# Three DMA queues instead of two for the backward part of a cached-attention decode kernel

## The chip, the cores and the metric

The kernel runs on one core of one Trainium2 chip. The time is device microseconds for one launch, and the number compared is the median of several executions. One further execution was recorded by the hardware profiler; all rows of a profile shown below come from such a recording. Engines are named as the profile names them: PE does matrix products (PEld loads their weights), DVE the element-wise work, ACT copies and activations, POOL (GpSimd) some small copies and some DMA issues, SP (SyncE) DMA issues only. Sixteen DMA engines move all data between device memory and the on-chip buffer.

## The reference

The forward pass is one decode step of a transformer block: layer norm, attention of one query per batch row and head against a cache of 4096 keys and values, then a gated feed-forward part. The kernel must give the output and, for a given gradient of the output, the gradients of eight inputs. Cut to what matters here:

```python
B, Sq, D = 4, 1, 512;  H, Sk, Dh = 32, 4096, 128          # bfloat16 throughout
q      = (layernorm(x) @ wq).reshape(B, Sq, H, Dh).transpose(0, 2, 1, 3)
scores = einsum("bhqd,bhkd->bhqk", q, k_cache) * Dh ** -0.5
p      = softmax(scores)
o      = einsum("bhqk,bhkd->bhqd", p, v_cache)
h      = x + o.transpose(0, 2, 1, 3).reshape(B, Sq, H * Dh) @ wo
out    = h + swiglu(layernorm(h), w1, w3, w2)
# returned: out and the vjp of out for x, k_cache, v_cache, wq, wo, w1, w3, w2
```

For each of the B x H = 128 heads, the gradient of the values is the outer product of p (4096 long) and the gradient dO of that head's output (128 long). The gradient of the keys is the outer product of dS and q, where dS = p * (V dO - c) * scale, with one number c per head. K, V, dK and dV are each 128 heads of 4096 x 128 numbers, 1 MB per head, so reading K once and V twice and writing dK and dV once is nearly all of the 708 MB that the kernel moves.

## The kernel before

The kernel has a forward part (up to about 690 us), a short middle part (the feed-forward part and its gradient), and a backward part that runs over the 128 heads, s = 0 to 127. The order of instructions on every engine is the order of the program text; each engine works through its own queue in that order and stops at an instruction whose wait isn't met.

On-chip memory is cut into 23 slots of 1 MB (lines 103 to 120). `Slot(...)` takes the oldest free slot from a list, and `give()` puts it back at the end. A slot that is taken again is written only when its last use has ended; for a slot that was stored, this means that the store has landed.

One head in the backward part goes as follows.

- `load_V2` (line 789) issues the load of a head's V (line 793) from SP. In the backward part the slots of V form a ring of seven (`NV2`, `vring`): `front` gives a slot back to the ring when the products that read it have been issued, and `prefetch` (line 1168), at the start of each step of the loop, loads the next head into it. Nine heads are loaded ahead before the loop starts (lines 801 and 873).
- `front(s)` (line 1140) transposes V of head s on PE in four groups of eight blocks (`V_T`, line 760), ACT copies each group back into the same slot (line 761), and PE multiplies it with dO in 32 small products (line 1148, tile `dP_ps`). `front` also asks POOL for `P_pairs` (line 1138), a copy of p in the form that DVE reads.
- `grad_V(s)` (line 773) lets DVE form the outer product p x dO in a slot `gv` (line 766) and stores it to `out_3`, the gradient of V, from POOL (line 777).
- `grad_K(s)` (line 1154) lets DVE form dS (lines 1158 and 1161) and the outer product dS x q in a slot `gk` (line 766) and stores it to `out_2`, the gradient of K, from POOL (line 1165).

In the loop (line 1175) the order is: prefetch, `front(s + 1)`, `grad_V(s + 1)`, `grad_K(s)`, and from step 2 on a piece of side work (`step`): first the rest of dO (lines 1103 to 1116), from step 21 on `side_work` (lines 947 to 1098), which makes the gradients of x and the five weight matrices. The side work issues some transfers of its own: loads of wq (line 977) and w2 (line 499) from SP, rearrangements of a few rows (lines 969, 1032 and 1072) from ACT, and the stores of the weight gradients from POOL.

Each transfer signals its end on one of sixteen semaphores that the compiler deals out in turn: eight for transfers issued from POOL, and eight shared by those issued from SP and ACT. A transfer that is dealt a semaphore waits, on the engine that issues it, until the transfer that had this semaphore before has landed. So at most eight transfers of each kind are under way at a time.

Of the kernel before, what the change touches and what calls it, by code (L numbers as in the profile page):

```python
# [24 lines left out]
def kernel(  # L25
# [22 lines left out]
    nc = tc.nc  # L48
# [35 lines left out]
    def bh_of(s):  # L84
        return s % B, s // B

    def rows_of(ap):
        return ap.rearrange("(p j) d -> p j d", p=P)

    def cache_head(ap, s):  # L90
        b, h = bh_of(s)
        return rows_of(ap[b, h])
# [82 lines left out]
    def ones_window(col):  # L175
# [11 lines left out]
                          in_=rowg[:, None, :, None].to_broadcast([P, 4, 8, 4]))  # L187
# [409 lines left out]
    def step(k, n=1):  # L597
        for _ in range(n):
            next(units[k], None)
# [150 lines left out]
    V2s, VTs = {}, {}  # L750
# [14 lines left out]
    def outer(dst, col2, row):  # L765
        nc.vector.tensor_tensor(  # L766
            out=dst.rearrange("p j (r t) -> p j r t", t=2),
            in0=col2[:, :, None, :].to_broadcast([P, SJ, Dh // 2, 2]),
            in1=row.rearrange("p (r t) -> p r t", t=2)[:, None, :, :].to_broadcast([P, SJ, Dh // 2, 2]),
            op=ALU.mult,  # L770
        )

    def grad_V(s):
        b, h = bh_of(s)
        gv = Slot("gv")
        outer(gv.heads(), P2s.pop(s), reps["rdo", s // REP][:, s % REP, :])
        nc.gpsimd.dma_start(out=rows_of(out_3[b, h]), in_=gv.heads())  # L777
        if s > 1:
            gv.give()
        else:  # L780
            first_gv.append(gv)
# [4 lines left out]
    vring = deque()  # L786
    nv = {"next": 0}

    def load_V2():
        s = nv["next"]  # L790
        if s < NH:
            V2s[s] = Slot("V2", vring if vring else free)
            nc.sync.dma_start(out=V2s[s].heads(), in_=cache_head(A_v_cache, s))
            nv["next"] += 1

    with ExitStack() as cm:
# [4 lines left out]
        while free:  # L801
            load_V2()
# [70 lines left out]
        while len(free) > 1:  # L873
            load_V2()
# [48 lines left out]
    with ExitStack() as c2:  # L923
# [216 lines left out]
        def front(s):  # L1140
            if s % REP == 0:
                replicate(s)
            if s not in VTs:
                V_T(s, psT)
            VT = VTs[s].heads()
            dP_ps = psD.tile([P, SJ], FP32, name="dP_ps", tag="dP")
            for j in range(SJ):
                nc.tensor.matmul(dP_ps[:, j:j + 1], lhsT=VT[:, j, :], rhs=dOT_bf[:, s:s + 1], start=True, stop=True)  # L1148
            sl = VTs.pop(s)
            (vring if len(V2s) + len(VTs) + len(vring) < NV2 else free).append(sl.i)  # L1150
            P_pairs(s + 2)
            bwd[s] = dP_ps

        def grad_K(s):
            b, h = bh_of(s)
            dP_ps = bwd.pop(s)
            t = bw3.tile([P, SJ], FP32, tag="dSt", name="dSt")
            nc.vector.tensor_scalar(out=t[:], in0=dP_ps[:], scalar1=c_rep[:, s:s + 1], scalar2=scale,  # L1158
                                    op0=ALU.subtract, op1=ALU.mult)
            dS2 = bw3.tile([P, SJ, 2], BF16, tag="dS2", name="dS2")  # L1160
            nc.vector.tensor_tensor(out=dS2[:], in0=t[:, :, None].to_broadcast([P, SJ, 2]),
                                    in1=P_all[:, s, :, None].to_broadcast([P, SJ, 2]), op=ALU.mult)
            gk = Slot("gk")
            outer(gk.heads(), dS2, reps["rq", s // REP][:, s % REP, :])
            nc.gpsimd.dma_start(out=rows_of(out_2[b, h]), in_=gk.heads())  # L1165
            gk.give()

        def prefetch():
            while nv["next"] < NH and vring:
                load_V2()  # L1170


        O0, S0 = 2, 21
# [1 line left out]
        for s in range(NH):  # L1175
            prefetch()
            if s + 1 < NH:
                if s + 1 not in V2s and s + 1 not in VTs:
                    load_V2()
                if s == 0:  # L1180

                    first_gv[0].give()
                front(s + 1)
                if s > 0:
                    grad_V(s + 1)
            grad_K(s)
            if s == 0:
                first_gv[1].give()
            if s >= S0:
                step("s", 1 if s < S0 + 38 else 3)  # L1190
            elif s >= O0:
                step("o")
# [31 lines left out]
```

## Time and profile before

| | |
|---|---|
| median of 4 executions | 1724.37 us (1723.57 to 1726.14) |
| the profiled execution's own time | 1724.0 us |
| its span, first to last instruction | 1721.7 us |
| moved | 707.87 MB, mean 411 GB/s over the span |
| of that, written | 282.34 MB |
| busy: PE, DVE, ACT, POOL | 77%, 73%, 56%, 26% of the span |
| copies of transposed V on ACT, line 761 | 512 of 1016 ns |
| outer products on DVE, line 766 | 125 + 128 of 2293 ns |
| issue of a dK or dV store on POOL | 256 of 533 ns |

The profile's rows of DMA queues name them by what issues them: `hardware_dynamic` q1 holds what SP issues, q10 what ACT issues, `software_dynamic` q0 what POOL issues. The DMA row in the list of 40 slices (43 us each) is the mean busy share of the sixteen DMA engines, in tenths. The span and the execution's own time differ by 2.3 us of start and end outside the instructions.

### The profile page before, as it was taken

To read this page: it belongs to the slowest core of one execution; us is meant where nothing else is said; L and a number is where in the kernel's file an instruction comes from. 1 tells how busy PE (TensorE), PEld (TensorE's weight loads), DVE (VectorE), ACT (ScalarE), POOL (GpSimd) and SP (SyncE) were. 2 spreads that over 40 slices of the span, in tenths; PEclk is the share of its full clock that TensorE was granted. 3 is DMA by queue.
4 is the path that set the end of the run, shared out by engine and by line. 5 is a ranking of instruction groups with operands and counts; after the bars stand their busy time and mean duration, and the time that the engine had idled before them with its cause. 6 is when DMAs were issued, how large, how long until landed. Compare 5 with 4: busy or idle time off the path is not lost.

```text
span 1721.7 us, 44279 instructions
## 1 busy us (share of the span) xinstructions
PE 1320.2 (77%) x19124; PEld 1117.2 (65%) x19124; DVE 1255.7 (73%) x1389; ACT 960.1 (56%) x1470; POOL 440.6 (26%) x808
## 2 busy tenths in 40 slices
PE   5888888888888888887687788767638777887760
PEld 4777776666667666876677777767636555665660
DVE  5899899899998997676766676665566456655582
ACT  3455444444454444677555555547637657777660
POOL 1221222222222231221122333322233232222221
PEclk8999999999999999666756655656866565555665
DMA  9999999999999999999999999999999999999996
GB/s 397 419 418 419 419 419 419 418 419 418 411 418 406 418 403 395 377 424 418 414 418 415 417 413 415 416 419 416 422 423 410 421 411 415 416 416 415 415 419 286
DMA packets 101867, 707.87 MB, mean 411 GB/s; under 512 B 11284, under 2 KB 15392, under 8 KB 17704
## 3 DMA queue, kind: packets, MB, share of 16 engines
q1 hardware_dynamic: 62272, 422.60, 59.5%
q0 software_dynamic: 39008, 282.37, 40.0%
q8 instruction: 150, 2.46, 0.5%
q14 instruction: 45, 0.37, 0.1%
q10 hardware_dynamic: 392, 0.07, 0.0%
HBM read 422.59 MB, written 282.34 MB: 409 GB/s over the span
## 4 chain that ended last, share of the span: by engine, by line
DMA 50%; PE 4%; DVE 4%; issue 2%; ACT 2%; POOL 0%; ACTq 0%; POOLq 0%; DVEq 0%
DMA out_dram<-gv 28%; DMA out_dram<-gk 22%; DVE gv L766 1%; DVE gk L766 1%; ACT V L761 1%; PE pt_tps L760 1%; PE M_ps L433 1%; DVE PK L418 1%; PE pt_w L562 0%; ACT Pn L397 0%; ACTq L1072 0%; PE kP_ps L443 0%; PE gps L942 0%; PE gu_ps L833 0%; PE pt_wo L571 0%
## 5 line engine op out<-in xcount | busy, mean ns | idle before, releaser
L761 ACT COPY V<-pt_tps 128x1024 bf16<-128x1024 bf16 x512 | 492.4, 1016 | 186.4 <-PE pt_tps L760 127.6
L760 PE MATMUL pt_tps<-ident_b,V 128*128 128x128 bf16 x4096 | 445.2, 289 | 60.4 <-ACT V L761 55.0
L760 PEld LDWEIGHTS <-V 128*128 128x128 bf16 x4096 | 393.8, 136 | 124.1 <-issue 116.5
L766 DVE TENSOR_TENSOR gv<-P,reps 128x4096 bf16<-128x4096 bf16 x125 | 286.7, 2293 | 207.2 <-DMA out_dram<-gv 74.4
L766 DVE TENSOR_TENSOR gk<-dS,reps 128x4096 bf16<-128x4096 bf16 x128 | 293.4, 2292 | 104.6 <-DMA out_dram<-gk 47.8
L433 PE MATMUL M_ps<-PK,Vn 128*128 128x130 bf16 x4096 | 287.7, 223 | 43.4 <-DMA Vn<-in_A_v_cache_dram 43.0
L418 DVE TENSOR_TENSOR PK<-Kn,PK 128x4096 bf16<-128x4096 bf16 x128 | 292.4, 2284 | 32.8 <-POOL PK L414 32.5
L433 PEld LDWEIGHTS <-Vn 128*128 128x128 bf16 x4096 | 254.6, 100 | 64.0 <-DMA Vn<-in_A_v_cache_dram 55.9
L325 DVE STREAM_TRANSPOSE KT<-Kn 128x512 f32<-128x512 f32 (+1 forms) x321 | 250.7, 797 | 0.3 <-issue 0.2
L320 ACT COPY KT<-pt_tps 128x1024 bf16<-128x1024 bf16 x128 | 129.5, 1012 | 189.1 <-PE pt_tps L319 153.1
L1148 PE MATMUL dP_ps<-dOT_bf,V 128*128 128x1 bf16 x4096 | 145.4, 165 | 108.3 <-DVE dSt L1158 58.6
L1148 PEld LDWEIGHTS <-V 128*128 128x128 bf16 x4096 | 137.5, 102 | 124.2 <-issue 64.4
L1165 POOL DMA_DIRECT2D out_dram<-gk x128 | 68.2, 533 | 392.9 <-DMA out_dram<-gk 144.5
L331 POOL TENSOR_TENSOR W<-qrep,wmask 128x128 bf16<-128x128 bf16 x128 | 123.2, 963 | 82.4 <-PE S_ps L351 67.8
L777 POOL DMA_DIRECT2D out_dram<-gv x128 | 68.4, 534 | 285.3 <-DVE dSt L1158 98.6
L414 POOL COPY PK<-P_all 128x64 bf16<-128x64 bf16 x128 | 32.6, 254 | 422.1 <-ACT P_all L408 419.1
L1138 POOL COPY P<-P_all 128x64 bf16<-128x64 bf16 x125 | 118.9, 951 | 0.0
L408 ACT COPY P_all<-pt_P 32x64 bf16<-32x64 bf16 x256 | 52.1, 203 | 60.0 <-PE pt_P L404 57.7
L319 PE MATMUL pt_tps<-ident_b,Kn 128*128 128x128 bf16 x1024 | 80.0, 222 | 0.0
L443 PE MATMUL kP_ps<-PK,onesw 128*32 128x512 bf16 x1024 | 79.5, 387 | 0.0
L319 PEld LDWEIGHTS <-Kn 128*128 128x128 bf16 x1024 | 61.6, 99 | 25.7 <-issue 25.6
L1129 ACT CAST reps<-rep_ps 128x512 bf16<-128x512 f32 x62 | 36.4, 587 | 72.7 <-PE rep_ps L1126 70.3
(237 smaller groups left out, 1349.6 us busy)
## 6 DMA issues: line engine op xcount, KB each, us to landing
Kn<-in_A_k_cache_dram SPq DMA_DIRECT2D x128, 1024.0 KB, 15.7
Vn<-in_A_v_cache_dram SPq DMA_DIRECT2D x128, 1024.0 KB, 16.0
V<-in_A_v_cache_dram SPq DMA_DIRECT2D x128, 1024.0 KB, 10.9
out_dram<-gv POOLq DMA_DIRECT2D x128, 1024.0 KB, 27.3
out_dram<-gk POOLq DMA_DIRECT2D x128, 1024.0 KB, 27.4
wq<-in_A_wq_dram SPq DMA_DIRECT2D x8, 1024.0 KB, 10.9
out_dram<-gw POOLq DMA_DIRECT2D x6, 896.0 KB, 27.9
wo<-in_A_wo_dram SPq DMA_DIRECT2D x4, 1024.0 KB, 12.4
```

Source lines behind the costliest of these rows:

```text
L319: nc.tensor.transpose(pt[:, i, :], Kn[:, c * GW + i, :], ident_b[:])
L320: nc.scalar.copy(out=KT[:, c * GW:(c + 1) * GW, :], in_=pt[:])
L325: nc.vector.transpose(out=KT[:, c * w_:(c + n) * w_], in_=Kn[:, c * w_:(c + n) * w_])
L331: nc.gpsimd.tensor_tensor(out=W[:, hl], in0=qrep[:, :, s:s + 1].to_broadcast([P, 4, 32]), in1=wmask[:, hl, None, :].to_broadcast([P, 4, 32 ...
L418: nc.vector.tensor_tensor(out=PK[:, :, 0:Dh].rearrange("p j (r t) -> p j r t", t=2), in0=Ks[s].heads().rearrange("p j (r t) -> p j r t", t=2),
L433: nc.tensor.matmul(hold["M"][:], lhsT=Vn[:, j, :], rhs=PK[:, j, :], start=(j == 0), stop=(j == SJ - 1))
L443: nc.tensor.matmul(hold["kP"][32 * q:32 * (q + 1), :, :], lhsT=ones_window(w), rhs=PK[:, j0:j0 + 4, 0:Dh], start=(w == 0 and c == 0), stop ...
L760: nc.tensor.transpose(pt[:, i, :], v[:, g * GW + i, :], ident_b[:])
L761: nc.scalar.copy(out=v[:, g * GW:(g + 1) * GW, :], in_=pt[:])
L766: nc.vector.tensor_tensor(out=dst.rearrange("p j (r t) -> p j r t", t=2), in0=col2[:, :, None, :].to_broadcast([P, SJ, Dh // 2, 2]), in1=r ...
L1138: nc.gpsimd.tensor_copy(out=P2s[s][:], in_=P_all[:, s, :, None].to_broadcast([P, SJ, 2]))
L1148: nc.tensor.matmul(dP_ps[:, j:j + 1], lhsT=VT[:, j, :], rhs=dOT_bf[:, s:s + 1], start=True, stop=True)
```

## The change

In the backward part three engines issue the large transfers, one kind each: the V loads that the loop asks for go from SP to ACT, the dK stores go from POOL to SP, and the dV stores stay on POOL. The nine V loads ahead of the loop stay on SP, since `load_V2` keeps SP as its default.

```diff
-    def load_V2():
+    def load_V2(eng=nc.sync):
         s = nv["next"]
         if s < NH:
             V2s[s] = Slot("V2", vring if vring else free)
-            nc.sync.dma_start(out=V2s[s].heads(), in_=cache_head(A_v_cache, s))
+            eng.dma_start(out=V2s[s].heads(), in_=cache_head(A_v_cache, s))
             nv["next"] += 1
...
             gk = Slot("gk")
             outer(gk.heads(), dS2, reps["rq", s // REP][:, s % REP, :])
-            nc.gpsimd.dma_start(out=rows_of(out_2[b, h]), in_=gk.heads())
+            nc.sync.dma_start(out=rows_of(out_2[b, h]), in_=gk.heads())
             gk.give()
 
         def prefetch():
             while nv["next"] < NH and vring:
-                load_V2()
+                load_V2(nc.scalar)
...
                 if s + 1 not in V2s and s + 1 not in VTs:
-                    load_V2()
+                    load_V2(nc.scalar)
```

PE and DVE keep their instructions and order. ACT gains 119 load issues, POOL loses 128 store issues, and SP loses the 119 loads and gains the 128 stores.

## The prediction

> **What bounds the kernel now.** I read the page's slices first, then its queues and its chain, then stretches of the span, then the waits of the queues that the change touches.
>
> ```profile
> span 1721.7 us, 44279 instructions
> ...
> DMA  9999999999999999999999999999999999999996
> GB/s 397 419 418 419 419 419 419 418 419 418 411 418 406 418 403 395 377 424 418 414 418 415 417 413 415 416 419 416 422 423 410 421 411 415 416 416 415 415 419 286
> ...
> q1 hardware_dynamic: 62272, 422.60, 59.5%
> q0 software_dynamic: 39008, 282.37, 40.0%
> ...
> DMA 50%; PE 4%; DVE 4%; issue 2%; ACT 2%; POOL 0%; ACTq 0%; POOLq 0%; DVEq 0%
> ```
>
> The DMA row is 9 until the last slice, and the two queues together fill 99.5% of sixteen engines' span. The chain that ended last is half DMA: stores of gv and gk, each holding a slot that DVE needs next. No compute engine is above 77%. So the time is bytes divided by the rate of the DMA engines, plus a start and an end. No byte changes, so the change can only act on the rate, on the end, or by letting the DMA engines run dry. The stretches, from the table of windows (busy times of PE, PEld, DVE, ACT and POOL, then clock, DMA share, GB/s):
>
> ```profile
> 86.00:430.00 344.00, 295.00 (x4904) 241.29 (x4901) 315.38 (x417) 175.24 (x385) 84.98 (x204) 0.99 1.01 419
> 731.00:1634.00 903.00, 677.16 (x8548) 584.49 (x8546) 576.04 (x485) 567.97 (x672) 247.62 (x358) 0.62 1.01 417
> 1290.00:1634.00 344.00, 266.19 (x3028) 207.80 (x3027) 206.19 (x167) 239.61 (x311) 94.59 (x136) 0.58 1.01 415
> 1640.00:1700.00 60.00, 29.82 (x456) 26.67 (x454) 43.94 (x36) 27.86 (x30) 13.89 (x31) 0.64 1.01 418
> 1700.00:1704.00 4.00, 0.00 (x0) 0.00 (x0) 0.00 (x0) 0.00 (x0) 0.06 (x1) 0.50 1.02 420
> 1704.00:1708.00 4.00, 0.00 (x0) 0.00 (x0) 0.00 (x0) 0.00 (x0) 0.00 (x0) 0.50 0.63 266
> 1708.00:1718.50 10.50, 0.00 (x0) 0.00 (x0) 0.00 (x0) 0.00 (x0) 0.00 (x0) 0.50 0.17 71
> ```
>
> Two losses are to be seen. Forward, with SP's loads alone, the rate is 419 GB/s; backward, with SP's loads and POOL's stores, 417 (415 in its second half) at the same full share. And the engines don't finish together: at 1704 the share falls from 1.02 to 0.63, then to 0.17, until about 1718. Some DMA engines end 14 us after the first ones, all of them working on POOL's stores, since the last V load is issued at 1640. The waits, and the issue times (minimum, median, maximum in ns):
>
> ```profile
> SPq L793 <- PE dP_ps L1148: 815.0, 112, 23.5
> SPq L977 <- DMA out_dram<-gk: 47.2, 3, 20.1
> SPq L977 <- DMA out_dram<-gv: 15.4, 1, 15.4
> POOL out_dram L1165 <- DMA out_dram<-gk: 144.5, 45, 4.7
> POOL out_dram L777 <- DMA out_dram<-gv: 98.1, 44, 4.1
> L793 SPq DMA_DIRECT2D V<-in_A_v_cache_dram x128: 327/328/1868, 676.4 to 1640.0; - x128
> V<-in_A_v_cache_dram SPq DMA_DIRECT2D x128, 1024.0 KB, 10.9
> out_dram<-gv POOLq DMA_DIRECT2D x128, 1024.0 KB, 27.3
> out_dram<-gk POOLq DMA_DIRECT2D x128, 1024.0 KB, 27.4
> ```
>
> SP is idle at the dP products: V loads run as far ahead as their ring allows and land in 10.9 us. POOL waits for its eighth-last store to land: stores are the backlog.
>
> **The change part by part.**
>
> V loads on ACT. 119 issues of 0.33 us (median of line 793 on SP) are 39 us of ACT's queue. ACT's own rows are of other, small shapes and dearer (the four oflat transfers took 0.48 to 1.76 us, median 1.52): 119 x 1.52 = 181 us. I take 0.33, the row with the same shape. ACT is idle for 903 - 568 = 335 us from 731 to 1634, so both ends are covered in sum; without cover the cost would be those 39 to 181 us. The wait moves too: the load waits for head s's dP products, and behind it on ACT stand the copies of head s + 1. They wait for transposes that follow dP(s) in PE's order, and eight of those take 0.6 to 1.0 us in the timeline, longer than 0.33. Cost 0.
>
> A second wait is new. SP and ACT share eight semaphores, so a V load waits for the transfer eight earlier on SP and ACT together, about four heads back. A head takes 3.15 MB / 417 GB/s = 7.5 us, so that is 30 us. For most loads the earlier one is a V load (10.9 us to landing): no wait. Following the order of the built program, for 18 of the 119 it is a dK store: 27.4 us median, 38.6 at most, so the wait is between 0 and 8.6 us. Behind it stand ACT's copies, and for those PE and DVE wait. But POOL has up to eight dV stores under way, 8 x 1.05 MB / 417 = 20 us of transfers, so the DMA engines don't run dry: cost 0; without that cover at most 18 x 8.6 = 155 us.
>
> dK stores on SP. POOL loses 128 x 0.53 = 68 us and the waits ahead of line 1165; DVE waited for POOL's copies (line 1138) only 9.5 us in all, so this gives nothing. On SP the stores now stand behind the four wq loads and two w2 loads of the side work, which wait for a slot: 47.2 + 15.4 us for wq, 20.1 at the longest, about the 20 us that dV covers. Cost 0, at most 63.
>
> Stores under way: POOL's eight become up to eight dV and about four dK. It changes the depth of a backlog that is never empty: 0.
>
> Rate and end. These are the two losses above, and the part where the trace has no row: no store of this size issued from SP. Uneven end: from 1704 to 1718.1, 266 x 4 + 71 x 10.5 = 1.81 MB move in 14.1 us; evenly, at 418, they take 4.3, so 9.8 us are lost. Rate: 903 x (1 - 417 / 419) = 4.3 us. If both belong to POOL's queue, they shrink with its bytes, of which dK is 134.2 of 282.4 MB, 48%: -4.7 and -2.1, together -6.8 us. Bounds: at best the rest goes as well, -14.1; at 0, stores cost the same from any queue; on the loss side, a third queue costs what the second seems to have cost, +4.3. I take -6.8, because the lag is seen only where POOL's stores alone are left, and 419 is the rate of the queue that dK moves to.
>
> The sum against the profiled execution: 1724.0 - 6.8 = 1717.2. It was 0.4 below the median, so 1717.6.
>
> Two statements of the Trainium skill bear on this, both in its page "DMA: Bandwidth & Descriptors". The section "Issuing engines are not separate DMA queues" says that transfers from SP, ACT and POOL share the same sixteen engines and that more issuers save issue time alone; by it the result is 1724.4, no change, and the full DMA share above speaks for it. The section "Latency and other measured facts" says that two of the engines are usually slower in traces, with the software descriptor rings as its best guess; the late finishers agree with that in kind, and by it part of the 9.8 us goes away with dK. No view here tells which engines finish late.
>
> **The rivals.**
>
> *Hidden anyway, 1724.4.* The late engines are late for another reason: in the forward part too the rate dips to 411 and 406 without any POOL store. The rate difference could be that of writes against reads: stores alone (1640 to 1700) ran at 418. Against it: that end is so long only here.
>
> *A third queue lowers the rate, 1728.7 (slower).* Place: each DMA engine between 731 and 1700. One more queue went with 419 to 417, and the second half has 415. The same step again is +4.3 us; by the 415 row, 969 x (1 - 415 / 419) = 9.3 us, 1733.7. It decides once the rate from 731 to 1634 falls below 416.
>
> *V comes late, 1734.* V has one of two queues with work now and needs a third of the bytes; with three it gets just its third. If the loads then fall behind, the last V lands near the end, and behind it stand four copies of 1.0 us, the dP products (about 1.2), dS (0.5) and an outer product (2.3) before the last store can start: some 8 us, plus about 5 to landing (the quickest landed in 4.5), with 2.5 us of that being transfer at full rate. This costs about 10 us. It decides if V lands later than some 30 us. Against it: seven slots of V, nine loads ahead.
>
> **How the numbers follow.** Forecast 0.45, hidden 0.25, third queue 0.18, late V 0.12. A difference of 0.2% (3.4 us) is about what a measurement can tell from none. Faster comes from the forecast alone, 0.45; same 0.25; slower 0.30, from the last two. The forecast's own range is 1710 to 1721. Over all cases I take 1709 to 1735: from all of both losses gone to the slower rivals' ends; about 0.1 is left out for a stall of ACT or of SP that does uncover the engines.
>
> **What would show it.** Right: q0 falls to about 148 MB; DMA stays 9; the rate from 731 to 1634 is 418 or more; the end after the first engine's finish takes some 9 us instead of 14; V loads land within 20 us. Wrong: a slice below 9 in the backward part, ACT waiting at line 793 for transfers with DMA share below 1, the rate under 416, or an end as long as now.

## The result, and the profile after

| | before | after |
|---|---|---|
| median | 1724.06 us (53 executions, 1721.35 to 1728.26) | 1721.95 us (33 executions, 1720.10 to 1726.75) |
| profiled execution | 1724.0 us, span 1721.7 | 1722.26 us, span 1720.5 |

The ratio is 0.9987, with a 95% interval of 0.9982 to 0.9992. So the change gains 2.1 us, 0.13%: a difference that 53 and 33 executions can tell from none, but less than the 0.2% that the prediction called "no change". The forecast was 1717.6 with a range of its own of 1710 to 1721, and "hidden anyway" was 1724.4: the result lies between the two, just outside the forecast's own range and inside the wide one of 1709 to 1735.

These are the rows of the page after that answer to those shown of before: the span, the DMA busy share and GB/s in 40 slices, the queues (packets, MB, share of sixteen engines) and the chain by engine.

```profile
span 1720.5 us, 44163 instructions
...
DMA  9999999999999999999999999998999999999996
GB/s 397 418 418 419 419 418 419 418 418 419 412 417 408 418 404 392 380 421 422 424 424 424 424 424 424 423 425 335 425 424 425 425 417 396 422 421 421 419 420 280
...
q1 hardware_dynamic: 63568, 432.04, 60.9%
q0 software_dynamic: 20576, 148.15, 20.5%
q10 hardware_dynamic: 17528, 124.86, 17.7%
q8 instruction: 150, 2.46, 0.5%
...
DMA 16%; DVE 3%; issue 2%; PE 1%; ACT 1%; POOL 0%; ACTq 0%; DVEq 0%; SPq 0%; POOLq 0%
```

The work did move: q0 has 148 MB in place of 282, and 125 MB of V loads are now ACT's. From slice 18 on most slices run at 422 to 425 GB/s, where before they ran at 413 to 419. But one slice fell to 335 with a DMA share of 8 tenths, and the last one to 280 from 286. The row of 150 packets named `instruction` was in the page before, too, and the prediction passed over it: by its kind it is the loading of the engines' programs, 2.46 MB / 150 = 16 KB a packet, and its count follows the number of PE's instructions in runs 7 to 9 (one packet for 256 instructions, matrix products and weight loads counted singly). The stretches, in the columns of the prediction's table (the last three are the clock, the DMA share and GB/s):

```profile
731.00:1634.00 903.00, 684.05 (x8483) 591.62 (x8482) 568.64 (x478) 563.55 (x668) 211.28 (x249) 0.59 1.00 417
731.00:1140.00 409.00, 328.28 (x4179) 304.33 (x4178) 282.80 (x237) 246.62 (x271) 111.16 (x118) 0.57 1.01 423
1160.00:1200.00 40.00, 11.57 (x150) 10.95 (x150) 8.95 (x9) 10.28 (x12) 3.87 (x4) 0.50 0.86 345
1290.00:1634.00 344.00, 260.82 (x2949) 200.56 (x2947) 203.36 (x166) 233.94 (x306) 70.90 (x100) 0.57 1.01 418
1700.00:1704.00 4.00, 0.00 (x0) 0.00 (x0) 0.06 (x1) 0.00 (x0) 0.00 (x0) 0.50 1.01 424
1704.00:1708.00 4.00, 0.00 (x0) 0.00 (x0) 0.00 (x0) 0.00 (x0) 0.00 (x0) 0.50 0.37 156
1708.00:1718.50 10.50, 0.00 (x0) 0.00 (x0) 0.00 (x0) 0.00 (x0) 0.00 (x0) 0.50 0.07 28
1710.00:1718.00 8.00, 0.00 (x0) 0.00 (x0) 0.00 (x0) 0.00 (x0) 0.00 (x0) 0.50 0.06 26
```

Three of the same stretches before:

```profile
731.00:1140.00 409.00, 322.24 (x4213) 295.70 (x4211) 278.96 (x234) 248.47 (x273) 110.67 (x166) 0.62 1.01 417
1160.00:1200.00 40.00, 30.87 (x422) 28.29 (x422) 22.29 (x19) 27.11 (x31) 10.79 (x15) 0.65 1.01 416
1710.00:1718.00 8.00, 0.00 (x0) 0.00 (x0) 0.00 (x0) 0.00 (x0) 0.00 (x0) 0.50 0.12 52
```

Three things are to be read here.

- **The rate rose.** From 731 to 1140 it went from 417 to 423 at the same full share. That is worth 409 x (1 - 417 / 423) = 5.8 us. Over the whole of 731 to 1634, though, both kernels have 417: the hole and the stretch behind it (417 from 1200 to 1290, where before had 422) take it back.
- **A hole opened** between 1160 and 1200: share 0.86, 345 GB/s.
- **The end is no shorter.** At 1704 both kernels drop from full share, and both end at about 1718. After the change less is left to move (156 x 4 + 28 x 10.5 = 0.92 MB instead of 1.81), but the time until the last byte is the same. From 1710 to 1718 the share is 0.06, which is one engine of sixteen, and the trace shows one chain of 8 KB packets there, each starting as the one ahead of it ends. This engine is behind all others and ends when the last one did before.

How far behind can be read from the trace: it records sixteen arrivals for every large transfer, by their count one for each engine. At the last store the last arrival came 5.3 us after the fifteenth before the change, and 10.3 us after the change. Below this is called the lead of the other fifteen.

What opened the hole is in the waits of the changed kernel and in ACT's timeline (start, duration; in brackets the idle time before and what ended it):

```profile
ACT V L761 <- DMA dqflat<-dqr_bf: 31.0, 1, 31.0
```

```profile
1152.52 1.93 ACT L761 COPY V<-pt_tps 128x1024 bf16<-128x1024 bf16 x2 [0.19 <-PE pt_tps L760]
1154.30 28.02 ACTq L969 DMA_DIRECT2D dqflat<-dqr_bf  x4
1185.07 0.33 ACTq L793 DMA_DIRECT2D V<-in_A_v_cache_dram  x1
1185.44 1.93 ACT L761 COPY V<-pt_tps 128x1024 bf16<-128x1024 bf16 x2 [30.99 <-DMA dqflat<-dqr_bf]
```

Line 969 issues four transfers of 8 KB from ACT. Before, they took 4.81 us of ACT's queue; now they take 28.02 us. The copies of V behind them stand still for 31 us, and in the stretch with the hole PE is busy for 11.57 us of 40, where before it was busy for 30.87. SP and ACT share eight semaphores, and these now hold the dK stores, which land in 22.4 us (median), and V loads, which land in 16.1, where before they held V loads landing in 10.9. That this is what the four transfers wait for is inferred from the order of issue; the profile only names the transfers that ended the wait.

### The profile page after: what moved, and what is told of

Read it like the earlier page. It is cut to its first block, busy times and chain, and to the rows that moved or that the text cites. A ratio compares the mean times of both kernels' runs of the same rounds, so it can differ in the third digit from the quotient of the medians.

```text
span 1720.5 us, 44163 instructions
## 1 busy us (share of the span) xinstructions
PE 1331.1 (77%) x19124; PEld 1128.1 (66%) x19124; DVE 1253.5 (73%) x1389; ACT 960.0 (56%) x1470; POOL 406.3 (24%) x680
## 3 DMA queue, kind: packets, MB, share of 16 engines
q8 instruction: 150, 2.46, 0.5%
## 5 line engine op out<-in xcount | busy, mean ns | idle before, releaser
L760 PE MATMUL pt_tps<-ident_b,V 128*128 128x128 bf16 x4096 | 453.1, 292 | 101.4 <-ACT V L761 96.4
L760 PEld LDWEIGHTS <-V 128*128 128x128 bf16 x4096 | 401.9, 137 | 165.9 <-issue 153.8
L1148 PE MATMUL dP_ps<-dOT_bf,V 128*128 128x1 bf16 x4096 | 149.9, 166 | 84.3 <-ACT V L761 58.3
L1148 PEld LDWEIGHTS <-V 128*128 128x128 bf16 x4096 | 140.1, 104 | 97.7 <-ACT V L761 68.6
L1138 POOL COPY P<-P_all 128x64 bf16<-128x64 bf16 x125 | 153.2, 1226 | 0.0
L1129 ACT CAST reps<-rep_ps 128x512 bf16<-128x512 f32 x62 | 36.4, 586 | 75.3 <-PE rep_ps L1126 48.0
L397 ACT ACTIVATE Pn<-E,rl 128x1024 bf16<-128x1024 f32 x64 | 73.7, 1152 | 3.3 <-DVE rl L394 3.2
## 6 DMA issues: line engine op xcount, KB each, us to landing
out_dram<-gk SPq DMA_DIRECT2D x128, 1024.0 KB, 22.4
V<-in_A_v_cache_dram ACTq DMA_DIRECT2D x119, 1024.0 KB, 16.1
```

Source lines behind the costliest of these rows:

```text
L760: nc.tensor.transpose(pt[:, i, :], v[:, g * GW + i, :], ident_b[:])
L1138: nc.gpsimd.tensor_copy(out=P2s[s][:], in_=P_all[:, s, :, None].to_broadcast([P, SJ, 2]))
```

## The experiments

Two theories stood after the result. **A**: the time is the bytes over the mean rate of sixteen engines plus an end, and the hole at 1160 gave back what the higher rate gained. **B**: one DMA engine is behind all others and never idle, so it alone sets the end. Fifteen engines may then get faster, or stand still for 6 us, and the time stays. Under B the engine is late because it carries something that the others don't, and the loading of PE's program is the candidate.

All kernels were measured over five rounds with the kernel before on the same chip, in four batches: runs 1 to 4, 5 to 7, 8 to 11, and 12. The kernel before had medians of 1724.08, 1723.70, 1724.10 and 1722.95 us in them. The ratio isn't that of the medians; where a few executions are far out, as one of 1737.96 us in run 5, the two differ.

**1. The four row transfers off ACT.** The changed kernel, with line 969 on POOL.

```diff
-                nc.scalar.dma_start(out=flat.b(HD)[b:b + 1, :], in_=dqr_bf[b::B, :])
+                nc.gpsimd.dma_start(out=flat.b(HD)[b:b + 1, :], in_=dqr_bf[b::B, :])
```

> The kernel after, with the four small rearrangements of dq rows (line 969) issued from POOL instead of ACT. In the kernel after, ACT stood 31.0 us at them, and the DMA share fell to 0.54 to 0.73 between 1180 and 1195, some 5.8 us of all engines' time. Theory A (the time is the mean rate of the sixteen DMA engines plus the end): that loss comes back, about 1722 - 5.8 = 1716 us. Theory B (one DMA engine is later than the others and never stopped, so it alone sets the end): the dip goes from the slices, but the time stays at 1722 within 1.5 us, and the stretch at the end in which the share is 0.06 (one engine of sixteen) gets longer than the 10 us of the kernel after.

Measured: 1723.17 us, ratio to before 0.9998 (0.9989 to 1.0007). The stretches of this kernel:

```profile
731.00:1140.00 409.00, 323.96 (x4204) 299.42 (x4202) 284.30 (x241) 247.80 (x272) 111.95 (x119) 0.60 1.01 424
1160.00:1200.00 40.00, 11.15 (x149) 10.29 (x149) 12.51 (x10) 10.18 (x12) 3.88 (x9) 0.57 1.00 420
1710.00:1718.00 8.00, 0.00 (x0) 0.00 (x0) 0.00 (x0) 0.00 (x0) 0.00 (x0) 0.50 0.06 25
```

The hole is gone (1.00, 420), so line 969 on ACT made it. The time isn't better, and again one engine alone works from 1710 to 1718. It is alone for longer, as was expected under B: the lead of the other fifteen is now 16.4 us. This speaks against A. The arrivals of the changed kernel say the same from the other side: ahead of the hole the last arrival of a dV store was 12.1 us later than the mean of the other fifteen, behind it 2.5 us (1158 and 1236 us). While fifteen engines waited, the last one caught up. Run 1 is less clean than it was meant to be: from 1200 to 1290 this kernel ran at 399 GB/s where the changed kernel ran at 417, so a part of the gain was lost again in other places.

**2. dK stores on SP alone.** V loads stay on SP.

```diff
-                load_V2(nc.scalar)
+                load_V2()
...
-                    load_V2(nc.scalar)
+                    load_V2()
```

> The kernel before, with only the dK stores moved from POOL to SP; the V loads stay on SP, so there are two queues as before. If fewer bytes in POOL's queue raise the rate: 420 GB/s or more from 731 to 1634, where before had 417. If the number of queues raises it: 417. Theory A: at 421 or more the time is at most 1724 - 8 = 1716 us, as no transfer of ACT stalls it. Theory B: 1721 to 1724 us, with one late engine at the end.

Measured: 1751.80 us, ratio 1.0160 (1.0146 to 1.0173). A stretch, a wait of SP and the time to landing of the V loads:

```profile
731.00:1634.00 903.00, 665.06 (x8325) 573.34 (x8322) 558.59 (x473) 552.81 (x655) 213.11 (x244) 0.62 1.00 404
```

```profile
SPq L793 <- DMA V<-in_A_v_cache_dram: 199.7, 54, 9.5
```

```profile
V<-in_A_v_cache_dram SPq DMA_DIRECT2D x128, 1024.0 KB, 29.3
```

No expected value was near. With V loads and dK stores issued by the same engine, the rate is 404 at full share, V lands in 29.3 us instead of 10.9, and SP now waits 199.7 us for V loads to land. The engines are counted busy and move less. The V loads also stand in SP's queue behind the dK stores, for which SP waits longer still: 267.7 us for DVE's products and 229.3 us for earlier dK stores to land. What in the mixture costs the time wasn't tried.

**3. V loads on ACT alone.** dK goes back to POOL.

```diff
-            nc.sync.dma_start(out=rows_of(out_2[b, h]), in_=gk.heads())
+            nc.gpsimd.dma_start(out=rows_of(out_2[b, h]), in_=gk.heads())
```

> The kernel after, with the dK stores back on POOL, so that only the V loads have moved, to ACT. If fewer bytes in POOL's queue raise the rate: 417 GB/s from 731 to 1634 as before, and 1724 us by both theories, if ACT doesn't stall. If a separate queue for the loads raises the rate: 421 or more, and by theory A 1716 us. If the new issues hold ACT up: slower than 1724 and slices below full DMA share.

Measured: 1723.10 us, ratio 0.9990 (0.9982 to 0.9999).

```profile
731.00:1140.00 409.00, 330.88 (x4206) 304.64 (x4205) 277.00 (x231) 248.09 (x272) 108.75 (x164) 0.57 1.01 416
```

The rate is 416, that of before. A queue of their own for the V loads does nothing for the rate; it only makes room for dK on SP without the loss of run 2.

**4. All stores on SP.** V on ACT as in the changed kernel, dV too on SP.

```diff
-        nc.gpsimd.dma_start(out=rows_of(out_3[b, h]), in_=gv.heads())
+        nc.sync.dma_start(out=rows_of(out_3[b, h]), in_=gv.heads())
```

> The kernel after, with the dV stores moved from POOL to SP as well; V loads on ACT. Only the stores of the weight gradients stay on POOL. If the late engine is late in POOL's queue only: it finishes with the others, the share falls from 1 to 0 within some 5 us, and the time is 1708 to 1714 us, unless ACT stalls more (V loads, dK and dV now share eight semaphores, so a V load waits for a transfer 2.7 heads or 20 us earlier, often a store). If the engine is late whatever the queue: 1720 to 1723 us, the end as long as in the kernel after. If ACT's stalls let the engines run dry: over 1724 us.

Measured: 1724.06 us, ratio 0.9999 (0.9990 to 1.0008). POOL's queue is nearly empty, and still:

```profile
731.00:1140.00 409.00, 313.26 (x4031) 290.44 (x4031) 274.20 (x231) 238.37 (x261) 16.38 (x58) 0.57 1.01 417
731.00:1634.00 903.00, 667.75 (x8341) 579.80 (x8341) 565.52 (x476) 554.54 (x657) 62.28 (x131) 0.59 1.01 414
1710.00:1718.00 8.00, 0.00 (x0) 0.00 (x0) 0.00 (x0) 0.00 (x0) 0.00 (x0) 0.50 0.30 125
```

Taking the last stores off POOL lowers the rate again (417 and 414). So the 423 of the changed kernel isn't what "fewer bytes on POOL" gives. Here the sixteen engines end closer together (share 0.30 after 1710), and the end hasn't moved: a third kernel with another mean rate and the same time.

**5 and 6. All stores on SP, V loads on POOL**; then the same with line 969 on POOL as in run 1.

```diff
-        nc.gpsimd.dma_start(out=rows_of(out_3[b, h]), in_=gv.heads())
+        nc.sync.dma_start(out=rows_of(out_3[b, h]), in_=gv.heads())
...
-                load_V2(nc.scalar)
+                load_V2(nc.gpsimd)
...
-                    load_V2(nc.scalar)
+                    load_V2(nc.gpsimd)
```

> The three kinds dealt out differently: V loads from POOL, dK and dV stores from SP, nothing large from ACT. A V load then waits only for V loads, and dK and dV share SP's semaphores with few others. If one DMA engine is late because of stores issued from POOL: no late engine, the share falls from 1 to 0 within some 5 us at the end, and the time is 1708 to 1716 us. If the late engine has the same extra work whatever the queues are: 1720 to 1724 us and again about 10 us at a share of 0.06 to 0.1. ACT may still stand at the dq rows (line 969) for some 20 us; by theory B that costs nothing.

> The kernel of the run before in this list with the dq rows (line 969) issued from POOL too. Theory B: within 1.5 us of that run, whatever its time is. Theory A: faster than that run by the share that its dip costs, up to 6 us.

Measured: 1722.53 us, ratio 1.0004 (0.9987 to 1.0022), and 1722.90 us, ratio 0.9998 (0.9987 to 1.0009). The first of the two:

```profile
731.00:1140.00 409.00, 331.74 (x4208) 305.94 (x4208) 279.19 (x235) 248.37 (x273) 50.68 (x117) 0.58 1.01 415
1710.00:1718.00 8.00, 0.00 (x0) 0.00 (x0) 0.00 (x0) 0.00 (x0) 0.00 (x0) 0.50 0.08 34
```

POOL issues no dK or dV store any more, yet the late finishers are there, working on SP's stores. Their lateness doesn't belong to POOL's queue of stores. The two runs are within 0.4 us of each other, but they don't decide between A and B: run 5 has no hole to take away (share 1.01 from 1160 to 1200).

**7 and 8. The dose of PE's instructions.** Run 1 with 8 in place of 32 products for dP of a head (each makes four equal columns, so dK is made from a quarter of V), and run 1 with each of the 32 products issued twice.

```diff
-            for j in range(SJ):
-                nc.tensor.matmul(dP_ps[:, j:j + 1], lhsT=VT[:, j, :], rhs=dOT_bf[:, s:s + 1], start=True, stop=True)
+            for j in range(0, SJ, 4):
+                nc.tensor.matmul(dP_ps[:, j:j + 4], lhsT=VT[:, j, :], rhs=dOT_bf[:, s:s + 1].to_broadcast([P, 4]), start=True, stop=True)
```

```diff
-            for j in range(SJ):
+            for j in [j for j in range(SJ) for _ in range(2)]:
```

> The kernel with the dq rows on POOL (1723.2 us), with the dP products of line 1148 cut from 32 to 8 a head: each is made for one block of V and written to four columns, so dS and dK are made from a quarter of the dP values. All transfers of data are the same; PE has 2 x 24 x 128 = 6144 fewer matrix instructions, about a third of its instructions in the backward part, and fetches fewer. The profile shows instruction fetches as transfers of their own (q8: 150 packets, 2.46 MB, 0.5% of the engines' span, each of 16 KB), each on a single DMA engine. If the late engine is late because it carries such fetches: q8 falls by some 24 packets and the time by 3 to 7 us, to 1716 to 1720. If the lateness comes from the software queue or from the engine itself: 1722 to 1724 us, unchanged, since PE isn't the bound.

> The other direction: the kernel with the dq rows on POOL (1723.2 us), with each dP product of line 1148 issued twice, so PE has 2 x 32 x 128 = 8192 more matrix instructions and no data transfer changes. If the fetches of PE's instructions make one DMA engine late, at the 9.4 us / 24 packets = 0.39 us a packet of the run with a quarter of the products: q8 rises from 150 to about 182 packets and the time by some 12 us, to 1734 to 1737 us, with the DMA row at 9 throughout. If that run was faster because PE had less to do: PE stays below 90% of the span here, and the time is 1723 to 1726 us.

Measured: 1713.75 us, ratio 0.9943 (0.9930 to 0.9956), and 1737.77 us, ratio 1.0078 (1.0065 to 1.0091). From the pages, PE's busy time and the queue of instructions, first with fewer products and then with more, and the stretch in which the last engine works alone:

```profile
PE 1272.2 (74%) x16052; PEld 1058.1 (62%) x16052; DVE 1253.5 (73%) x1389; ACT 960.2 (56%) x1470; POOL 397.4 (23%) x684
...
q8 instruction: 126, 2.06, 0.5%
```

```profile
1704.00:1708.00 4.00, 0.00 (x0) 0.00 (x0) 0.00 (x0) 0.00 (x0) 0.00 (x0) 0.50 0.06 27
```

```profile
PE 1424.9 (82%) x23220; PEld 1235.6 (71%) x23220; DVE 1253.5 (72%) x1389; ACT 961.0 (55%) x1470; POOL 402.3 (23%) x684
...
q8 instruction: 182, 2.98, 0.7%
```

```profile
1718.00:1730.00 12.00, 0.00 (x0) 0.00 (x0) 0.00 (x0) 0.00 (x0) 0.00 (x0) 0.50 0.07 31
```

With 24 packets of instructions fewer the time falls by 9.4 us, 0.39 us for each; with 32 more it rises by 14.6 us, 0.46 for each. The last engine works alone until 1708 in the one and until 1730 in the other. The packets are 0.4 and 0.5 MB of 708, under 0.08%, and the time moved by 0.5 and 0.8%. In the trace a packet lasts 1.0 us, so 24 of them over sixteen engines would be 1.5 us: no mean gives 9.4. The lead of the other fifteen falls from 16.4 us in run 1 to 4.8 in run 7, and it is 16.8 in run 8. There the others are later too: from 1200 to 1290 the share was 0.96 at 377 GB/s.

**9. Fewer instructions, but more work for PE.** Run 7, and the transposes of V made by 8 in place of 32 products of a head, each four times as wide. Here too dK is made from a part of V alone.

```diff
-            pt = ps.tile([P, GW, P], BF16, tag="tps", name="pt_tps")
-            for i in range(GW):
-                nc.tensor.transpose(pt[:, i, :], v[:, g * GW + i, :], ident_b[:])
-            nc.scalar.copy(out=v[:, g * GW:(g + 1) * GW, :], in_=pt[:])
+            for i in range(0, GW, 4):
+                pt = ps.tile([P, 4, P], FP32, tag="tps", name="pt_tps")
+                nc.tensor.matmul(pt[:], lhsT=v[:, g * GW + i, :], rhs=ident_b[:, None, :].to_broadcast([P, 4, P]), start=True, stop=True)
+                nc.scalar.copy(out=v[:, g * GW + i:g * GW + i + 4, :], in_=pt[:])
```

> The kernel with the dq rows on POOL, with few PE instructions in the backward part: 8 dP products a head as in the run with a quarter of the products, and V's 32 transposes a head replaced by 8 products of one block with four identities side by side (same columns through PE, so about the same PE time), copied by ACT as 8 copies of 128x512. PE's matrix instructions fall from 128 to 32 a head, dK is wrong, all data transfers are the same. Expected if fetches set the end: q8 near 102 packets; at 0.39 us a packet 1723 - 19 = 1704, but not below what the other engines allow, so 1703 to 1709 us. Otherwise 1714 (as with a quarter of the products) or more.

Measured: 1705.81 us, ratio 0.9894 (0.9881 to 0.9906).

```profile
PE 1360.0 (80%) x12980; PEld 784.4 (46%) x12980; DVE 1255.7 (74%) x1389; ACT 1015.6 (60%) x1982; POOL 407.9 (24%) x684
...
q8 instruction: 102, 1.67, 0.4%
```

PE is busier than in run 7 (1360 us against 1272) and ACT too; only the number of instructions is smaller. The time falls by another 7.9 us for 24 packets. So it follows the packets, not PE's busy time. (The packets and PE's instructions change together in all these runs; what is said of the one holds of the other.) The lead is now 2.8 us, so little is left to gain from this engine alone.

The lateness can also be watched as it grows. Between about 876 and 1145 us the last arrival of the dV stores falls further and further behind the mean of the other fifteen:

| | packets of instructions per 100 us | last engine falls behind, us per 100 us |
|---|---|---|
| run 8 | 10.7 | 3.3 |
| changed kernel | 7.9 | 2.4 |
| run 1 | 7.9 | 2.3 |
| run 7 | 5.2 | 1.3 |
| run 9 | 2.6 | 1.6 |
| run 12 | 2.5 | 1.2 |

Three things limit what this shows. With few packets (runs 9 and 12) the engine still falls behind, so not all of it goes with them. In the kernels with dK and dV in one queue the order doesn't hold: the kernel before, run 11 and run 10 show 1.3, 0.2 and 3.4 us per 100 us at 7.5, 5.1 and 2.5 packets, and more than one engine is late there. And it isn't shown that this engine moves the packets itself: in the changed kernel 21 of them, of 0.88 to 0.97 us each, fall into this stretch, and from one dV store to the next the engine never falls back by more than 0.40 us. Runs 9 and 12 have one larger step each, of 1.7 and 1.8 us. What comes with a packet and delays this one engine is open.

**10, 11 and 12. What the change is worth with fewer instructions.** The kernel before with both cuts, the kernel before with the dP cut alone, and the changed kernel itself with both cuts, line 969 left on ACT. The edits are those of runs 7 and 9.

> The kernel before with the same two cuts of PE instructions. Here both kinds of store are issued from POOL, the rate was 417, and several engines ended between 1704 and 1712. If the change's gain in rate is real and only hidden by the engine that carries the fetches: 1709 to 1714 us, 4 to 8 us more than the run above. If the change gives nothing but balance: the same time as the run above within 2 us.

> The kernel before with the dP products alone cut to 8 a head (24 fewer fetches expected). If the engine that carries the fetches sets the end in the kernel before as well: about 1724 - 9 = 1715 us, 1713 to 1717, near the 1713.75 us of the three-queue kernel with the same cut. If before is bound by the mean rate of its engines: 1721 to 1724 us.

> The changed kernel itself, the four small row transfers left on ACT, with both cuts of PE work: eight products for dP and eight for the transposes of a head, so that dK is made from a part of V alone. It is the pair to the kernel before with the same two cuts (1720.1 us), and tells how much of the 14 us between that kernel and the changed one with both cuts and the rows moved (1705.8) belongs to the change alone. If the change alone brings the gain and the stall of ACT is hidden: 1704 to 1709 us, 102 packets in the queue of instructions. If the stall of ACT counts as soon as the last DMA engine is no longer behind: 1705.8 + 5 to 7 = 1711 to 1713. If the gain belonged to the move of the rows: about 1720.

Measured: 1720.07 us, ratio 0.9986 (0.9971 to 1.0001); 1720.89 us, 0.9982 (0.9973 to 0.9992); 1707.76 us, 0.9904 (0.9888 to 0.9921). Stretches of the kernel before with both cuts, and of the changed kernel with both:

```profile
731.00:1140.00 409.00, 335.28 (x1430) 144.91 (x1430) 277.05 (x233) 267.72 (x491) 118.46 (x165) 0.50 1.01 414
1710.00:1718.00 8.00, 0.00 (x0) 0.00 (x0) 0.00 (x0) 0.00 (x0) 0.00 (x0) 0.50 0.15 63
```

```profile
731.00:1140.00 409.00, 336.63 (x1437) 144.93 (x1436) 280.78 (x237) 269.75 (x495) 110.53 (x117) 0.50 1.01 425
1160.00:1200.00 40.00, 18.75 (x97) 8.45 (x94) 19.60 (x16) 18.29 (x33) 8.48 (x8) 0.54 0.95 374
1694.00:1698.00 4.00, 0.00 (x0) 0.00 (x0) 0.00 (x0) 0.00 (x0) 0.00 (x0) 0.50 0.50 211
1698.00:1702.00 4.00, 0.00 (x0) 0.00 (x0) 0.00 (x0) 0.00 (x0) 0.00 (x0) 0.50 0.09 37
```

This is where the expected gain was:

| packets of instructions | before | changed | gain, us |
|---|---|---|---|
| 150 | 1724.06 | 1721.95 | 2.1 |
| 126 | 1720.89 | 1713.75 (line 969 on POOL) | 7.1 |
| 102 | 1720.07 | 1707.76 | 12.3 |

The same change gains 12.3 us when the program is shorter, although its share falls to 0.95 at the row transfers. The last two rows compare kernels of different batches; each against the kernel before of its own batch, the gains are 6.7 and 11.2 us. In the kernel before, by contrast, fewer instructions bring 3.2 and 4.0 us: its other engines are late as well. The lead of the other fifteen was only 5.3 us before, so not much more than that could be gained from the last engine alone; with fewer instructions it is 2.7 and 3.0. In the changed kernel with both cuts it is 4.4. (The profiled execution of the kernel before with both cuts took 1723.1 us, 3 more than its median, so its share of 0.15 after 1710 is that of a long one.) So before the change more than one engine holds the end; the change takes the others away from it, and the one whose lateness follows the packets then stands alone. With both cuts, the row transfers cost at most about 2 us more on ACT than on POOL (1707.76 against 1705.81).

## Why the prediction was right and wrong

**What was right.** The time fell and is inside the wide range, but that range also held the rivals, and the forecast's own range was missed by 1 us. The sum of -6.8 came out at -2.1 from terms that were wrong in both directions, so the hit is partly luck. No compute engine was the bound, and q0 fell to 148 MB. V loads landed in 16.1 us (within 20), and line 793 was issued in 0.33 us. Of the signs named for being wrong two appeared: a slice below 9 and an end as long as before; and the rate from 731 to 1634, which was to be 418 or more, was 417.

**The step that failed is "Rate and end", in its term of the uneven end, -4.7 us.** It gave all late finishing to POOL's queue and let it shrink with that queue's bytes. By the prediction's own working, 0.92 MB in 14.1 us, evenly 2.2 us, leaves 11.9 us lost: the term measured +2.1 instead of -4.7. The late engines were of two sorts. Fifteen ended 5.3 to 13.6 us ahead of the last one before, and 10.3 to 18.9 us ahead of it with dK off POOL. The very last one did not end earlier, and its lateness follows the packets of instructions (runs 7 to 9), not POOL's stores (runs 5 and 6). "The lag is seen only where POOL's stores alone are left" was true of the trace, but it is the wrong inference: at the end of this kernel nothing but those stores was left for any engine to be late with.

**The term of the rate, -2.1 us, was too small, and its reason was wrong.** From 731 to 1140 the gain was 5.8 us. The working took 419, the rate of the forward loads, as the limit; the changed kernel runs at 422 to 425 in most slices; and over the whole of 731 to 1634 nothing was left of the gain. And the rate isn't POOL's share of the bytes: all stores on SP (run 4) gives 417 and 414, and V alone on its own queue (run 3) 416. Of the splits tried, only dK and dV in two queues, with V in a third, is faster. The packets' own times in the trace say where the rate goes: from 731 to 1140 an 8 KB packet took 316.5 ns on average before and 311.5 after. Most take 309 ns. In a queue that holds dK and dV together, 5.6 to 7.2% take over 330 ns (POOL's before and in run 3, SP's in runs 4 and 5); in the changed kernel's three queues, 0.9 to 2.8%. In run 2 it is 6.2% in both queues. Why these packets take longer is open.

**ACT at cost 0 missed its place.** The new wait on the shared semaphores was found, but sought only at the V loads and on SP; it struck hardest at line 969, whose four transfers are issued from ACT. At line 793 it showed too. These are ACT's waits whose end let line 793 issue and then the instruction named (total, times, longest):

```profile
ACT V L761 <- DMA out_dram<-gk: 8.0, 1, 8.0
ACT reps L1129 <- DMA V<-in_A_v_cache_dram: 21.3, 6, 3.6
ACT V L761 <- DMA V<-in_A_v_cache_dram: 16.4, 5, 3.4
```

Behind dK stores ACT stood there for 8.0 us and, ahead of L1129, for 5.2 us, within the 8.6 us of the working. Behind earlier V loads, for which the working had "no wait", it stood eleven times, 37.7 us in all. In these stretches (731 to 1140 and 1290 to 1634) the DMA share stayed at 1.01, so there the cover held. "ACT waiting with a DMA share below 1" was named as a sign of being wrong, at line 793; it came at line 969. There the 20 us of cover were used up: the wait was 31 us, and the share fell. The lost transfer is 40 x (1 - 345 / 416) = 6.8 us by the rate of before in that stretch. It didn't lengthen the kernel as far as run 1 can tell, since the last engine set the end.

**The rivals.** "Hidden anyway" came closest in outcome and in kind: its first sentence, that the late engines are late for another reason, is what the runs showed of the last one. "A third queue lowers the rate" fell: from 731 to 1140 the rate rose, and over 731 to 1634 it was the same. "V comes late" fell at 16.1 us, but run 2 shows how near it lay: with dK and V in one queue V lands in 29.3 us, and the kernel is 1.6% slower.

**The two statements of the Trainium skill**, page "DMA: Bandwidth & Descriptors". "Issuing engines are not separate DMA queues" says that more issuers save issue time alone; by the total that is right within 0.2%, but the rate of 423 against 417 from 731 to 1140, and the 12.3 us with a shorter program, go against it. "Latency and other measured facts" gives the software descriptor rings as its best guess for why two engines are usually slower. That isn't what these runs show of the last one: with 13.92 MB on POOL's queue (run 4) the kernel ends at the same time.

**What stays open.** Which DMA engine is last, and what ties it to the packets: the 150 packets of the changed kernel last 150.6 us together, 1.0 us each, two to three times the 0.33 to 0.46 us that one costs in time, and the arrivals don't show them on that engine. Why two kinds of large transfer in one queue lower the rate. And a version with fewer PE instructions and the full dK wasn't made, so no kernel with the complete result beat the changed one.

## What to carry to other kernels

Where the DMA share is full until the end, look at how the engines finish: a share of 0.06 over the last microseconds is one engine of sixteen, and a gain in the mean rate didn't move it here. Look at what else the DMA engines move besides the data, the loading of the instruction streams first; here fewer and larger instructions on PE, which wasn't the bound, bought time. Before large transfers go to an engine's queue, list every small transfer that the engine issues: four of them held up the work behind them for 31 us here.

## What the runs showed of the hardware that wasn't expected

- The time goes with the loading of the program, and out of proportion to its bytes: with 24 packets of 16 KB fewer it fell by 9.4 and then 7.9 us, with 32 more it rose by 14.6 us, in a kernel that moves 708 MB.
- With dK and dV in two queues, one DMA engine of sixteen falls steadily behind, by 1.2 to 3.3 us per 100 us, the most where there are the most such packets, and yet in steps too small for the packets themselves (at most 0.40 us in the changed kernel, where a packet takes 0.88 us or more).
- One queue for V loads and dK stores ran at 404 GB/s at full share; two queues of pure loads and pure stores ran at 417; three queues, with the two kinds of stores apart, ran at 423 to 425 from 731 to 1140, ahead of the stall.
- Four transfers of 8 KB took 28.02 us of ACT's queue, where they had taken 4.81, once SP and ACT issued large stores and loads; that the shared semaphores tie the two together is inferred.
